# Retention and mixture-of-depths on one core: smaller loads, a one-pass rank, later weights, and a third MLP held back

## The chip, the cores and the metric

The kernel runs on one core of a Trainium2 chip. A core has five engines, each with its own stream of instructions: TensorE (PE, matrix products into PSUM; loads of its stationary operand are listed apart as PEld), VectorE (DVE), ScalarE (ACT), GpSimd (POOL) and SyncE (SP), which here only issues transfers. Sixteen DMA engines move data between HBM and the on-chip SBUF. The metric is the device time of one execution in microseconds (us), lower is better.

## The reference

Eight sequences of 576 tokens, 8 heads of width 64, everything in float32. First retention without a softmax, then a mixture of depths over the 512 channels that the heads form together: the 128 tokens of each sequence with the highest score pass through a two-layer MLP, weighted by a sigmoid of their score; the others stay as they are.

```python
scores = q @ k.T / sqrt(64)                     # per batch and head, 576x576
gamma  = 1 - 2.0 ** (-5 - arange(8))            # one decay a head
ret    = scores * where(i >= j, gamma ** (i - j), 0)
x      = (ret @ v) laid out as (8, 576, 512)
s      = x @ w_gate                             # one score a token
top    = the 128 tokens of a sequence with the highest s
out    = x;  out[top] += sigmoid(s[top]) * (relu(x[top] @ w1) @ w2)   # w1 512x1024, w2 1024x512
```

## The kernel before

**Tiling.** A sequence is cut into 9 chunks of 64 tokens. Two sequences, a pair, lie side by side on the 128 partitions (64 each), so there are 4 pairs of 9 chunks, 36 steps in all. The host packs for each step the transposed q, the transposed k, v and k into one row of 4 x 512 floats a partition, 1 MB a step.

**A retention step** (`s` counts them) does on PE, in 128 matmuls of 64x64: the scores of the chunk with itself (`sc_ps`, L142), the running state `u_ps` from k and v (L152), and for the chunk before it the product of masked scores and v (`y_ps`, L162) and of q and the state (L169). POOL scales v by the decay (`vs`, L130), DVE masks the scores (`am`, L185), scales the result (`xs`, L199) and forms the score with `wg` (L203); ACT copies the state out of PSUM (L192). SP stores `xs` (L205).

**Ranking.** When a pair is through, `spread` puts its 576 scores in a row on all partitions (L218, L222), `compare` counts per chunk on DVE how many scores of the row are higher (L228) and, in a second instruction over 64 to 576 columns, how many equal ones come before (L231); `one_hot` adds the two counts (L237) and compares them with 128 slots (L240). `fetch` turns that into row numbers on PE (`idx_ps`, L252, L253) and has POOL gather the chosen rows from the output in HBM (`xr`, L261); `gates` recomputes their scores (L274, L276).

**MLP.** A pair's MLP is cut into nine parts that wait in a list, `parts`: one `turn` (transposes, L289), four `up` (16 matmuls each, L300), four `down` (8 matmuls each, L312), the second and fourth of which end with the addition (L317) and POOL's scatter into the output (L319).

**Order.** The order of instructions on PE, DVE, ACT and SP is the order of the code. The last loop goes through the steps: a load six steps ahead, the step's matmuls, masks and stores, then one part from the list if there is one, then what `steps` holds for that step. For pair `p`, with `s = 9p + 10`, that is `spread` at `s`, three `compare` at each of `s`, `s+1`, `s+2`, `one_hot` at `s+2`, `fetch` at `s+3`, `gates` at `s+4`; the pair's nine parts join the list at `s+5`, so that the first is taken a step later. After step 36 there is no retention left. SP issues loads, weights and stores in one queue: `load(s+6)`, a weight matrix at two of the steps, then the store of step `s-1`, which waits for DVE. Loads have 8 buffers. The compiler gives the transfers issued by SP eight semaphores in turn, so a transfer waits until the one eight before it has landed.

Of the kernel before, what the change touches and what calls it, by code (L numbers as in the profile page):

```python
# [9 lines left out]
F32 = mybir.dt.float32  # L10
# [3 lines left out]
OP = mybir.AluOpType  # L14
PSUM = bass.MemoryType.PSUM

P = 128
C = 64
ET = mybir.EngineType
# [3 lines left out]
def layout(H, NC, cap):  # L23

    at, n = {}, 0
    for name, size in (("dec", 2 * NC * H), ("causal", C), ("ident", C), ("before", NC * C),
                       ("slots", cap), ("eye", P), ("place", 2 * NC + 2)):
        at[name] = n
        n += size
    at["end"] = n  # L30
    return at
# [3 lines left out]
def kernel(  # L35
# [22 lines left out]
    nc = tc.nc  # L58
# [32 lines left out]
    def load(s):  # L91
        x = loads.tile([P, 4, DM], F32, name="raw")
        nc.sync.dma_start(out=x, in_=qkvk[s].rearrange("p (a e) -> p a e", a=4))
        raw[s] = x

    ctx.enter_context(tc.manual_schedule(engines=ENGINES))
    load(0)
    table = const.tile([P, col["end"]], F32, name="table")
    n_first = col["ident"]
    nc.sync.dma_start(out=table[:, :n_first], in_=consts[:, :n_first])  # L100
    load(1)
    load(2)
# [10 lines left out]
    ident = table[:, col["ident"] : col["ident"] + C]  # L113
    before = table[:, col["before"] : col["before"] + NC * C]
    slots = table[:, col["slots"] : col["slots"] + cap]
# [95 lines left out]
    def spread(p):  # L211
        row[p] = work.tile([P, S], F32, name="row", bufs=2)
        for c0 in range(0, NC, 8):
            t = bank("row_ps")
            c1 = min(c0 + 8, NC)
            for c in range(c0, c1):
                for half in halves:
                    nc.tensor.matmul(  # L218
                        t[half, C * (c - c0) : C * (c - c0) + C],
                        sc[p][half, c : c + 1].to_broadcast([C, C]), ident[half, :],  # L220
                        start=True, stop=True, skip_group_check=True)
            nc.scalar.copy(out=row[p][:, C * c0 : C * c1], in_=t[:, : C * (c1 - c0)])  # L222
        rank[p] = work.tile([P, 2, NC], F32, name="rank", bufs=2)

    def compare(p, c):
        s = sc[p][:, c : c + 1]
        scr = work.tile([P, S], F32, name="scr2", bufs=1)
        nc.vector.tensor_scalar(scr, row[p], s, None, op0=OP.is_gt, op1=OP.add,  # L228
                                accum_out=rank[p][:, 0, c : c + 1])
        end = C * c + C  # L230
        nc.vector.scalar_tensor_tensor(  # L231
            scr[:, :end], row[p][:, :end], s, before[:, S - end :],
            op0=OP.is_equal, op1=OP.mult, accum_out=rank[p][:, 1, c : c + 1])

    def one_hot(p):
        r = work.tile([P, NC], F32, name="r", bufs=2)
        nc.vector.tensor_tensor(out=r, in0=rank[p][:, 0, :], in1=rank[p][:, 1, :], op=OP.add)  # L237
        hot[p] = work.tile([P, NC, cap], BF16, name="hot", bufs=nb)
        for c in range(NC):
            nc.vector.tensor_scalar(hot[p][:, c, :], slots, r[:, c : c + 1], None,  # L240
                                    op0=OP.is_equal)
# [97 lines left out]
    for p in range(NP):  # L339
# [6 lines left out]
        at(s + 4, gates, p)  # L346
        at(s + 5, mlp, p)

# [6 lines left out]
    for s in range(last + 1):  # L355
        if s + AHEAD < NS:
            load(s + AHEAD)
        if s == 4:
            nc.sync.dma_start(out=w1_sb, in_=w1.rearrange("(a p) f -> p a f", p=P))
        if s == 7:  # L360
            nc.sync.dma_start(out=w2_sb, in_=w2.rearrange("(a p) d -> p a d", p=P))
# [80 lines left out]
```

## Time and profile before

| | us |
|---|---|
| three runs | 299.83, 296.64, 299.77 (median 299.77) |
| the profiled execution | 298.31 |
| its span, first to last instruction | 296.5 |

| engine | busy us | share of the span |
|---|---|---|
| PE | 236.4 | 80% |
| PEld | 182.1 | 61% |
| DVE | 144.3 | 49% |
| POOL | 54.3 | 18% |
| ACT | 39.5 | 13% |

The profile is of one execution. Busy times are summed over instructions; matmuls are pipelined and their ends are modelled, so a busy PE need not be working at its peak. The mean clock granted to TensorE was 0.886 of full speed. In the lists an idle time is put down to whatever signal came last before it ended; "issue" means that the engine waited for nothing that the profile shows. A number in brackets after x counts instructions.

### The profile page before, as it was taken

What the parts mean: (1) busy time and instruction counts of PE and PEld (TensorE: products, weight loads), DVE (VectorE), ACT (ScalarE), POOL (GpSimd) and SP (SyncE); (2) the same over time, 40 slices, a digit from 0 to 9 for tenths busy, and PEclk for the clock granted to TensorE, in tenths of its full rate; (3) what the DMA queues carried; (4) which work ended last, traced back from release to release, by engine and by line L of the source; (5) the groups of instructions that cost most, each with busy time, mean ns of one, the idle gap of its engine ahead of it and who ended that gap; (6) DMA issues with size and microseconds to landing.
All of it is one profiled execution on the core that took longest, in us unless ns stands there. A gap on an engine that the chain in (4) does not pass through costs nothing.

```text
span 296.5 us, 10844 instructions
## 1 busy us (share of the span) xinstructions
PE 236.4 (80%) x4984; PEld 182.1 (61%) x4984; DVE 144.3 (49%) x361; ACT 39.5 (13%) x74; POOL 54.3 (18%) x56
## 2 busy tenths in 40 slices
PE   2575547555649889999799999988999994999992
PEld 2464447554547778875656888646568861468640
DVE  0152225346895834399754343996643089310011
ACT  1010001001100411310021122100220110011100
POOL 1231112211114212111242211113310000310011
PEclk9996577778655799999799999997999998799998
DMA  7999997997555898546396954112321100300000
GB/s 284 363 423 422 413 401 277 349 403 267 181 179 190 296 366 287 187 127 234 122 326 233 349 189 179 38 38 76 110 106 38 38 0 0 106 35 2 0 35 35
DMA packets 13693, 57.11 MB, mean 193 GB/s; under 512 B 1488, under 2 KB 1616, under 8 KB 9040
## 3 DMA queue, kind: packets, MB, share of 16 engines
q1 hardware_dynamic: 12368, 52.22, 47.4%
q0 software_dynamic: 1280, 4.20, 4.1%
q8 instruction: 39, 0.64, 0.8%
q14 instruction: 6, 0.05, 0.0%
HBM read 44.88 MB, written 11.53 MB: 190 GB/s over the span
## 4 chain that ended last, share of the span: by engine, by line
PE 55%; DVE 22%; issue 14%; DMA 5%; ACT 1%; SPq 1%; POOLq 0%; POOL 0%; DVEq 0%
PE h_ps L300 16%; PE ye_ps L312 10%; DVE scr L228 9%; PE sc_ps L142 7%; PE u_ps L152 7%; DVE scr L231 6%; PE y_ps L162 6%; PE y_ps L169 5%; DMA table<-in_consts 3%; DMA xr<-out,idx 2%; DVE am L185 2%; PE idx_ps L252 2%; PE row_ps L218 1%; DVE scr L203 1%; DVE xs L199 1%
## 5 line engine op out<-in xcount | busy, mean ns | idle before, releaser
L142 PE MATMUL sc_ps<-raw 64*64 64x64 f32 x1152 | 55.4, 255 | 15.6 <-issue 10.1
L162 PE MATMUL y_ps<-vs,am 64*64 64x64 f32 x1152 | 53.5, 253 | 16.7 <-DVE am L185 8.5
L130 POOL TENSOR_TENSOR vs<-raw,table 128x512 f32<-128x512 f32 x36 | 38.1, 1059 | 134.5 <-PE y_ps L162 81.0
L142 PEld LDWEIGHTS sc_ps<-raw 64*64 64x64 f32 x1152 | 49.2, 167 | 20.6 <-issue 15.0
L162 PEld LDWEIGHTS y_ps<-vs,am 64*64 64x64 f32 x1152 | 47.6, 164 | 21.4 <-issue 11.5
L312 PE MATMUL ye_ps<-w_sb,hT 128*128 128x512 f32 x128 | 59.4, 614 | 0.0
L300 PE MATMUL h_ps<-xg,w_sb 128*128 128x256 f32 x256 | 58.5, 384 | 0.7 <-ACT xg L290 0.7
L152 PE MATMUL u_ps<-vs,raw 64*64 64x64 f32 x1024 | 51.4, 259 | 7.9 <-issue 7.7
L300 PEld LDWEIGHTS h_ps<-xg,w_sb 128*128 128x128 f32 x256 | 47.6, 190 | 7.7 <-ACT xg L290 1.0
L152 PEld LDWEIGHTS u_ps<-vs,raw 64*64 64x64 f32 x1024 | 45.9, 171 | 9.9 <-issue 9.8
L169 PE MATMUL y_ps<-st,raw 64*64 64x64 f32 x1024 | 48.6, 252 | 4.2 <-issue 4.1
L169 PEld LDWEIGHTS y_ps<-st,raw 64*64 64x64 f32 x1024 | 43.1, 164 | 5.1 <-issue 5.1
L199 DVE TENSOR_TENSOR xs<-y_ps,table 128x512 f32<-128x512 f32 x36 | 24.8, 688 | 39.7 <-PE y_ps L169 39.7
L312 PEld LDWEIGHTS ye_ps<-w_sb,hT 128*128 128x128 f32 x128 | 24.2, 195 | 27.1 <-issue 26.4
L185 DVE TENSOR_TENSOR am<-sc_ps,table 128x512 f32<-128x512 f32 x36 | 24.8, 689 | 31.5 <-PE y_ps L162 21.2
L228 DVE TENSOR_SCALAR_CACHE_REDUCE scr<-row,sc 128x576 f32<-128x576 f32 x36 | 29.2, 812 | 20.2 <-ACT row L222 19.2
L192 ACT COPY st<-u_ps 128x512 f32<-128x512 f32 x32 | 18.8, 586 | 150.4 <-PE y_ps L169 120.6
L203 DVE SCALAR_TENSOR_TENSOR scr<-xs,wg 128x512 f32<-128x512 f32 x36 | 24.9, 692 | 1.2
L319 POOL DMA_INDIRECT out<-o,idx x8 | 8.1, 1011 | 93.9 <-DVE idx L257 52.4
L231 DVE SCALAR_TENSOR_TENSOR scr<-row,sc,table 128x64 f32<-128x64 f32 (+8 forms) x36 | 22.3, 620 | 1.3
L317 DVE SCALAR_TENSOR_TENSOR o<-ye_ps,gate,xr 128x512 f32<-128x512 f32 x8 | 6.0, 750 | 33.3 <-PE ye_ps L312 33.3
L302 ACT ACTIVATE hT<-h_ps 128x512 f32<-128x512 f32 x16 | 9.6, 598 | 57.6 <-PE h_ps L300 57.6
(27 smaller groups left out, 81.6 us busy)
## 6 DMA issues: line engine op xcount, KB each, us to landing
raw<-in_qkvk SPq DMA_DIRECT2D x36, 1024.0 KB, 6.7
out<-xs SPq DMA_DIRECT2D x36, 256.0 KB, 2.6
w_sb<-in_w SPq DMA_DIRECT2D x2, 2048.0 KB, 12.3
table<-in_consts SPq DMA_DIRECT2D x1, 458.0 KB, 9.5
wg<-in_w_gate SPq DMA_DIRECT2D x1, 256.0 KB
xr<-out,idx POOLq DMA_INDIRECT x8, 4.3
out<-o,idx POOLq DMA_INDIRECT x8, 2.8
table<-in_consts SPq DMA_DIRECT2D x1, 104.0 KB, 5.0
```

Source lines behind the costliest of these rows:

```text
L130: nc.gpsimd.tensor_tensor(out=heads(vs[s]), in0=heads(raw[s][:, 2, :]), in1=dec[:, 0, c, :].unsqueeze(2).to_broadcast([P, H, D]), op=OP.mult,)
L142: yield lambda h=h, half=half: nc.tensor.matmul(sc_ps[s][half, hd[h]], x[half, 1, hd[h]], x[half, 0, hd[h]], start=True, stop=True, skip_g ...
L152: yield lambda h=h, half=half: nc.tensor.matmul(u[half, hd[h]], x[half, 3, hd[h]], vs[s][half, hd[h]], start=c == 0 and h == 0, stop=c == ...
L162: yield lambda h=h, i=i, half=half: nc.tensor.matmul(y_ps[s][halves[1 - i], hd[h]], am[s][half, h, :], vs[s][half, hd[h]], start=h == 0, s ...
L169: yield lambda h=h, i=i, half=half: nc.tensor.matmul(y_ps[s][halves[1 - i], hd[h]], raw[s][half, 0, hd[h]], st[s - 1][half, hd[h]], start= ...
L185: nc.vector.tensor_tensor(out=am[s], in0=heads(sc_ps[s]), in1=causal.unsqueeze(1).to_broadcast([P, H, C]), op=OP.mult)
L199: nc.vector.tensor_tensor(out=heads(xs[s]), in0=heads(y_ps[s]), in1=dec[:, 1, c, :].unsqueeze(2).to_broadcast([P, H, D]), op=OP.mult)
L203: nc.vector.scalar_tensor_tensor(scr, xs[s], 1.0, wg, op0=OP.mult, op1=OP.mult, accum_out=sc[p][:, c : c + 1])
L228: nc.vector.tensor_scalar(scr, row[p], s, None, op0=OP.is_gt, op1=OP.add, accum_out=rank[p][:, 0, c : c + 1])
L231: nc.vector.scalar_tensor_tensor(scr[:, :end], row[p][:, :end], s, before[:, S - end :], op0=OP.is_equal, op1=OP.mult, accum_out=rank[p][: ...
L300: nc.tensor.matmul(t[:, a, :w], w1_sb[:, d, P * (f + a) : P * (f + a) + P], xg[group][:, d, :w], start=d == 0, stop=d == KD - 1)
L312: nc.tensor.matmul(ye[u][:m], hT[group][:, f, at : at + m], w2_sb[:, f, :], start=f == 0, stop=f == FB - 1)
```

## The change

Four things change. A step's load is issued as four transfers, one for each of the packed arrays, into the same tile (`load`); the first table of constants now goes ahead of the first load. The two instructions of `compare` become one `scalar_tensor_tensor` over all 576 columns, which subtracts the score and compares the difference with 0 or with minus 2**-125 from a table `ahead` (1,088 columns in place of 576); the addition in `one_hot` falls away. The loads of `w1` and `w2` are issued at steps 7 and 10 in place of 4 and 7. The parts of a pair join the list at `s+4` in place of `s+5`, except those of the third pair (`p == 2`), which join at step 36.

```diff
--- before.py
+++ after.py
@@ -15,6 +15,7 @@
 PSUM = bass.MemoryType.PSUM

 P = 128
+TINY = 2.0**-125
 C = 64
 ET = mybir.EngineType
 ENGINES = {ET.PE, ET.DVE, ET.Activation, ET.SP}
@@ -23,7 +24,7 @@
 def layout(H, NC, cap):

     at, n = {}, 0
-    for name, size in (("dec", 2 * NC * H), ("causal", C), ("ident", C), ("before", NC * C),
+    for name, size in (("dec", 2 * NC * H), ("causal", C), ("ident", C), ("ahead", (2 * NC - 1) * C),
                        ("slots", cap), ("eye", P), ("place", 2 * NC + 2)):
         at[name] = n
         n += size
@@ -90,14 +91,15 @@

     def load(s):
         x = loads.tile([P, 4, DM], F32, name="raw")
-        nc.sync.dma_start(out=x, in_=qkvk[s].rearrange("p (a e) -> p a e", a=4))
+        for a in range(4):
+            nc.sync.dma_start(out=x[:, a, :], in_=qkvk[s, :, a * DM : a * DM + DM])
         raw[s] = x

     ctx.enter_context(tc.manual_schedule(engines=ENGINES))
-    load(0)
     table = const.tile([P, col["end"]], F32, name="table")
     n_first = col["ident"]
     nc.sync.dma_start(out=table[:, :n_first], in_=consts[:, :n_first])
+    load(0)
     load(1)
     load(2)
     nc.sync.dma_start(out=table[:, n_first:], in_=consts[:, n_first:])
@@ -111,7 +113,7 @@
     dec = table[:, : 2 * NC * H].rearrange("p (s c h) -> p s c h", s=2, c=NC)
     causal = table[:, col["causal"] : col["causal"] + C]
     ident = table[:, col["ident"] : col["ident"] + C]
-    before = table[:, col["before"] : col["before"] + NC * C]
+    ahead = table[:, col["ahead"] : col["slots"]]
     slots = table[:, col["slots"] : col["slots"] + cap]
     eye = table[:, col["eye"] : col["eye"] + P]
     place = const.tile([P, NC + 1, 2], BF16, name="place")
@@ -220,24 +222,19 @@
                         sc[p][half, c : c + 1].to_broadcast([C, C]), ident[half, :],
                         start=True, stop=True, skip_group_check=True)
             nc.scalar.copy(out=row[p][:, C * c0 : C * c1], in_=t[:, : C * (c1 - c0)])
-        rank[p] = work.tile([P, 2, NC], F32, name="rank", bufs=2)
+        rank[p] = work.tile([P, NC], F32, name="rank", bufs=2)

     def compare(p, c):
-        s = sc[p][:, c : c + 1]
+
         scr = work.tile([P, S], F32, name="scr2", bufs=1)
-        nc.vector.tensor_scalar(scr, row[p], s, None, op0=OP.is_gt, op1=OP.add,
-                                accum_out=rank[p][:, 0, c : c + 1])
-        end = C * c + C
         nc.vector.scalar_tensor_tensor(
-            scr[:, :end], row[p][:, :end], s, before[:, S - end :],
-            op0=OP.is_equal, op1=OP.mult, accum_out=rank[p][:, 1, c : c + 1])
+            scr, row[p], sc[p][:, c : c + 1], ahead[:, (NC - 1 - c) * C :][:, :S],
+            op0=OP.subtract, op1=OP.is_gt, accum_out=rank[p][:, c : c + 1])

     def one_hot(p):
-        r = work.tile([P, NC], F32, name="r", bufs=2)
-        nc.vector.tensor_tensor(out=r, in0=rank[p][:, 0, :], in1=rank[p][:, 1, :], op=OP.add)
         hot[p] = work.tile([P, NC, cap], BF16, name="hot", bufs=nb)
         for c in range(NC):
-            nc.vector.tensor_scalar(hot[p][:, c, :], slots, r[:, c : c + 1], None,
+            nc.vector.tensor_scalar(hot[p][:, c, :], slots, rank[p][:, c : c + 1], None,
                                     op0=OP.is_equal)


@@ -344,7 +341,7 @@
         at(s + 2, one_hot, p)
         at(s + 3, fetch, p)
         at(s + 4, gates, p)
-        at(s + 5, mlp, p)
+        at(max(s + 4, NS) if p == NP - 2 else s + 4, mlp, p)

     AHEAD = 6
     for s in range(3, AHEAD):
@@ -355,9 +352,9 @@
     for s in range(last + 1):
         if s + AHEAD < NS:
             load(s + AHEAD)
-        if s == 4:
+        if s == 7:
             nc.sync.dma_start(out=w1_sb, in_=w1.rearrange("(a p) f -> p a f", p=P))
-        if s == 7:
+        if s == 10:
             nc.sync.dma_start(out=w2_sb, in_=w2.rearrange("(a p) d -> p a d", p=P))
         if s + 1 < NS:
             scaled(s + 1)
@@ -408,9 +405,9 @@
     table[:, : col["causal"]] = np.stack([1.0 / power, power / math.sqrt(D)], 1).reshape(P, -1)
     j = np.arange(C)
     table[:, col["causal"] : col["ident"]] = i[:, None] <= j[None, :]
-    table[:, col["ident"] : col["before"]] = i[:, None] == j[None, :]
-    table[:, col["before"] : col["slots"] - C] = 1.0
-    table[:, col["slots"] - C : col["slots"]] = j[None, :] < i[:, None]
+    table[:, col["ident"] : col["ahead"]] = i[:, None] == j[None, :]
+    table[:, col["ahead"] : col["ahead"] + S - C] = -TINY
+    table[:, col["ahead"] + S - C : col["ahead"] + S] = -TINY * (j[None, :] < i[:, None])
     table[:, col["slots"] : col["eye"]] = np.arange(cap)[None, :]
     table[:, col["eye"] : col["place"]] = np.eye(P)

```

**SP, from the first store on** (a transfer and what it waits for; DMAHW0 to DMAHW7 are the eight semaphores of its transfers). Before:

```order
L205 DMA out<-xs 128x512 [waits DMAHW3_49,DVE_49]
L93 DMA raw<-in_qkvk 128x2048 [waits DMAHW4_49,PE_49,Pool_49]
L205 DMA out<-xs 128x512 [waits DMAHW5_49,DVE_49]
L93 DMA raw<-in_qkvk 128x2048 [waits DMAHW6_49,PE_49,Pool_49]
L205 DMA out<-xs 128x512 [waits DMAHW7_49,DVE_49]
L93 DMA raw<-in_qkvk 128x2048 [waits DMAHW0_49,PE_49,Pool_49]
L359 DMA w_sb<-in_w 128x4x1024 [waits DMAHW1_49]
```

The same place in the changed kernel:

```order
L207 DMA out<-xs 128x512 [waits DMAHW3_49,DVE_49]
L95 DMA raw<-in_qkvk 128x512 [waits DMAHW4_49,PE_49,Pool_49]
L95 DMA raw<-in_qkvk 128x512 [waits DMAHW5_49]
L95 DMA raw<-in_qkvk 128x512 [waits DMAHW6_49]
L95 DMA raw<-in_qkvk 128x512 [waits DMAHW7_49]
L207 DMA out<-xs 128x512 [waits DMAHW0_49,DVE_49]
```

A load of one transfer has become four, each with the wait for the transfer eight before it; eight transfers now hold under two steps' loads, where they held about four steps' loads and stores.

**PE, where retention ends** (`sc_ps` to `y_ps` are retention, `xg_ps` the turn, `h_ps` and `ye_ps` the halves of the MLP, `row_ps` the spread of the fourth pair). Before, the end of step 35 and what follows up to the fourth pair's `idx_ps`:

```order
L142 MATMUL sc_ps<-raw 64x64 x2
L162 MATMUL y_ps<-vs,am 64x64 x2
L169 MATMUL y_ps<-st,raw 64x64 x16
L300 MATMUL h_ps<-xg,w_sb 128x256 x8
L162 MATMUL y_ps<-vs,am 64x64 x16
L169 MATMUL y_ps<-st,raw 64x64 x16
L300 MATMUL h_ps<-xg,w_sb 128x256 x16
L218 MATMUL row_ps<-table,sc 64x64 x18
L300 MATMUL h_ps<-xg,w_sb 128x256 x8
L312 MATMUL ye_ps<-w_sb,hT 128x512 x8
```

The same place in the changed kernel:

```order
L144 MATMUL sc_ps<-raw 64x64 x2
L164 MATMUL y_ps<-vs,am 64x64 x2
L171 MATMUL y_ps<-st,raw 64x64 x16
L164 MATMUL y_ps<-vs,am 64x64 x16
L171 MATMUL y_ps<-st,raw 64x64 x16
L286 MATMUL xg_ps<-table,xr 128x128 x8
L220 MATMUL row_ps<-table,sc 64x64 x18
L297 MATMUL h_ps<-xg,w_sb 128x256 x24
```

The third pair's turn and first `up` have moved behind the last retention matmul, and steps 33 to 35 have no part of an MLP between them; `idx_ps` of the fourth pair now follows the third `up`, and the last `up` and all `down` follow `idx_ps`.

**DVE, one step in which a pair is ranked** (`am`, `xs`, `scr,sc` are retention, `rank<-row` the comparison). Before:

```order
L185 TENSOR_TENSOR am<-sc_ps,table 128x512
L199 TENSOR_TENSOR xs<-y_ps,table 128x512
L203 SCALAR_TENSOR_TENSOR scr,sc<-xs,wg 128x512
L228 TENSOR_SCALAR scr_2681,rank<-row,sc 128x576
L231 SCALAR_TENSOR_TENSOR scr_2681,rank<-row,sc,table 128x256
L228 TENSOR_SCALAR scr_2684,rank<-row,sc 128x576
L231 SCALAR_TENSOR_TENSOR scr_2684,rank<-row,sc,table 128x320
L228 TENSOR_SCALAR scr_2687,rank<-row,sc 128x576
L231 SCALAR_TENSOR_TENSOR scr_2687,rank<-row,sc,table 128x384
```

In the changed kernel:

```order
L187 TENSOR_TENSOR am<-sc_ps,table 128x512
L201 TENSOR_TENSOR xs<-y_ps,table 128x512
L205 SCALAR_TENSOR_TENSOR scr,sc<-xs,wg 128x512
L230 SCALAR_TENSOR_TENSOR scr_2769,rank<-row,sc,table 128x576
L230 SCALAR_TENSOR_TENSOR scr_2771,rank<-row,sc,table 128x576
L230 SCALAR_TENSOR_TENSOR scr_2773,rank<-row,sc,table 128x576
```

Six instructions between two masks have become three.

## Rows read from the trace of the kernel before

**Rows 1.** The page, DMA queues: packets, MB, share of 16 engines.

```profile
q1 hardware_dynamic: 12368, 52.22, 47.4%
q8 instruction: 39, 0.64, 0.8%
```

**Rows 2.** The windows, stages of the span; the head names the columns.

```profile
core 0: us, PE busy (x) PEld busy (x) DVE busy (x) ACT busy (x) POOL busy (x), PEclk, DMA share, GB/s
0.00:73.20 73.20, 38.72 (x1367) 36.94 (x1367) 25.26 (x55) 7.86 (x13) 15.02 (x18) 0.81 0.94 365
73.20:99.20 26.00, 18.53 (x578) 16.75 (x580) 20.19 (x55) 3.63 (x5) 6.27 (x6) 0.57 0.56 189
228.74:296.50 67.76, 57.99 (x238) 36.84 (x238) 20.27 (x59) 6.37 (x13) 5.90 (x6) 0.93 0.08 28
```

**Rows 3.** The windows, from one restart of PE to the next.

```profile
19.39:25.84 6.45, 2.20 (x127) 2.07 (x127) 1.99 (x4) 0.59 (x1) 1.04 (x1) 0.88 1.01 419
25.84:32.11 6.27, 3.81 (x127) 3.62 (x127) 2.08 (x4) 0.59 (x1) 1.04 (x1) 0.50 1.02 418
44.67:48.49 3.82, 3.67 (x129) 3.58 (x128) 2.08 (x4) 0.59 (x1) 1.04 (x1) 0.55 0.53 218
54.39:61.37 6.98, 4.04 (x128) 3.85 (x128) 2.77 (x5) 0.00 (x0) 2.09 (x2) 0.76 1.02 389
66.83:73.19 6.36, 2.77 (x127) 2.64 (x127) 3.91 (x13) 1.29 (x3) 1.04 (x1) 0.92 0.83 303
73.19:76.87 3.68, 3.67 (x127) 3.50 (x127) 2.69 (x7) 0.59 (x1) 0.23 (x1) 0.50 0.16 56
```

**Rows 4.** The chain of waits in order of time: start us, us, what.

```profile
18.02 1.36 issue
...
21.59 4.25 issue
...
29.65 2.46 issue
```

**Rows 5.** DMA issues on the page: op, count, KB each, us to landing.

```profile
raw<-in_qkvk SPq DMA_DIRECT2D x36, 1024.0 KB, 6.7
out<-xs SPq DMA_DIRECT2D x36, 256.0 KB, 2.6
```

**Rows 6.** Groups by form: count | busy us, mean ns | idle before.

```profile
L228 DVE TENSOR_SCALAR_CACHE_REDUCE scr<-row,sc 128x576 f32<-128x576 f32 x36 | 29.2, 812 | 20.2 <-ACT row L222 19.2
L231 DVE SCALAR_TENSOR_TENSOR scr<-row,sc,table 128x576 f32<-128x576 f32 x4 | 3.3, 818 | 0.1
L231 DVE DVE_READ_ACCUMULATOR scr<-row,sc,table 128x1 f32 x36 | 2.9, 81 | 0.0
```

**Rows 7.** Group of the page, all forms of the second comparison together.

```profile
L231 DVE SCALAR_TENSOR_TENSOR scr<-row,sc,table 128x64 f32<-128x64 f32 (+8 forms) x36 | 22.3, 620 | 1.3
```

**Rows 8.** Timeline of DVE: start, us, instruction, idle before it and its releaser.

```profile
12.34 0.18 DVE L120 CAST place<-table 128x20 bf16<-128x20 f32 x1 [12.34 <-DMA table<-in_consts]
```

**Rows 9.** The windows, single steps between 99 and 229 us.

```profile
112.86:118.52 5.66, 5.66 (x113) 4.90 (x113) 2.28 (x5) 1.19 (x2) 1.03 (x2) 1.00 0.78 265
143.60:149.35 5.75, 4.66 (x131) 3.97 (x129) 3.10 (x8) 0.00 (x0) 2.45 (x3) 0.70 0.67 224
```

**Rows 10.** The chain of waits, MLP work of PE and the end.

```profile
112.86 3.65 PE h_ps L300 x16
...
161.72 1.02 PE xg_ps L289 x8
...
253.08 8.70 PE ye_ps L312 x16
...
277.46 6.88 PE ye_ps L312 x16
```

**Rows 11.** Waits of PE: waited for, us in total, times, longest.

```profile
PE idx_ps L252 <- DVE hot L240: 9.8, 4, 3.9
```

## The prediction, as put on record before the changed kernel's time was known

> **What bounds the kernel now.** I read the windows first, then the chain of waits, then the groups. By stage [rows 2] the first 73.2 us hold ten of the 36 steps and have the DMA engines busy at 0.94, while PE shows 38.7 us of work; this is the costliest stretch. It looks like a transfer limit, but it isn't one: loads run six steps ahead, and the chain there names no load as what PE waits for. It says "issue", that is nothing visible, for 1.4 to 4.3 us at a time [rows 4].
>
> Cutting the stretch where PE restarts shows what that is [rows 3]: each piece holds 127 to 129 matmuls and as many weight loads, some 256 instructions, whatever they are. The page has a queue named instruction with 39 packets and 0.64 MB [rows 1]: 16.4 KB a packet, and PE's 2 x 4984 instructions over 39 are 256 each. So I read the gaps as PE out of instructions until its next packet has come. A retention step is 4 x 32 matmuls with their weight loads, exactly one packet. [...]
>
> What a packet costs depends on what else the DMA engines carry [rows 3]. With DMA busy at 0.16 a piece takes 3.68 us, at 0.53 it takes 3.82, with loads in the way 6.27, and while the 2 MB of `w2` pass 6.98. The excess over 3.68 is 2.59 us with loads; 1 MB at the 418 GB/s of that row lasts 2.51 us. So the packet seems to wait for about one whole transfer in front of it, not for the whole queue: at 19.39 us SP had issued 10.5 MB and 17.4 us at 419 GB/s had moved 7.3, so 3.2 MB or 7.7 us were still queued, and that piece took 6.45 us, 2.77 over.
>
> From 99 us on the MLP parts fill the pieces (a step with an `up` is 5.66 us [rows 9], of which the `up` is 3.65 [rows 10], so retention alone is 2.01 on PE) and PE is the bound, except where it waits for the ranks: four times, 9.8 us in all, 3.9 at most [rows 11]. The tail after the last retention matmul is 67.76 us [rows 2].
>
> **The change, part by part.** The sum is against the profiled execution, 298.31 us, which is a span of 296.5 and 1.8 around it; the median of the three runs is 1.5 higher, inside their spread.
>
> *Loads in four.* Each transfer is 256 KB, 0.63 us at 418 GB/s. If a packet waits for one transfer, a piece becomes 3.68 + 0.63 = 4.31 us. Nine pieces lie between 19.39 and 73.19, 53.8 us together (the first and the last are in [rows 3]). One of them now meets `w1`; I give it the 6.98 us of the row with `w2`. 8 x 4.31 + 6.98 = 41.5: **-12.3 us**. Bounds: nine pieces of 3.68 are 33.1, -20.7 us; if the wait is for something that four transfers don't shorten, 6.27 stays and the gain is 0. I take the value near the better end, since the row with 0.53 is at 3.82. Two things speak for one transfer as the unit: the 2 MB one cost more than the 1 MB ones, and the wait did not grow with the queue. What the rows can't tell is whether the four transfers of a load count as one. [...] No row here shows the engines one by one.
>
> SP issues 144 loads in place of 36, at about 0.4 us each; with a store that is some 2 us a step against pieces of 4.31, so this is covered, and would show only in steps shorter than 2 us. The wait for the transfer eight before is now a wait with 2 MB in flight, 5 us of traffic, against 2.6 us to landing for a lone 256 KB store [rows 5]: covered too. Behind it the first store and `load(8)` go out some 4 us later than now, since SP must first get rid of the 32 initial pieces; `xs` has four buffers and `load(8)` is needed six pieces later, so nobody waits.
>
> At the start, DVE's first mask sits behind the cast of `place`, which waits for the second table until 12.34 us [rows 8]. That table grows by 512 columns, 256 KB, +0.63 us, and all bytes ahead of it come in rows of 2 KB, which ran at 389 in place of 419 GB/s [rows 3]: on 4 MB +0.7. Against that the gap of 1.36 us before the first restart [rows 4] goes. **0**, bounds -1.4 and +1.4.
>
> *Ranks in one pass.* A chunk costs now 812 + 620 ns and two accumulator reads of 81 [rows 6, 7], 1.59 us; the new instruction is that of the 576-column form, 818 + 81 = 0.90. Nine chunks: 6.2 us less on DVE for each pair, more than the longest of the four waits. **-9.8 us** on PE; bounds -9.8 and, if PE merely arrives earlier too, -5.
>
> [...] In the tail the 16 matmuls of `down` right behind the wait took 8.70 us, later ones 6.88 [rows 10]: **-1.8**.
>
> Between 73.2 and 99.2 us DVE holds the first pair's steps; 6.2 less 3.9 already counted leaves -2.3, but `w2` now passes here, 6.98 - 4.31 = 2.7: **+0.4**, bounds -2.3 and +2.7.
>
> *Weights later.* `w1` and `w2` are first read at steps 16 and 20, nine and ten steps after their issue, over 35 us: nobody waits for them. What they cost is counted above.
>
> *Third MLP held.* PE's matmuls stay the same; what counts is how many steps run bare, without a part. Steps 33 to 35 and half of 36 do now, and a bare step takes a packet's time, not 2.01: 3.5 x (3.68 - 2.01) = **+5.8** (no loads are left by then). Bounds: 0 if packets come faster, +8.0 at 4.31. Step 15 is no longer bare and takes the first pair's turn, 1.02 us [rows 10]: **-1.0**. In the tail the row of scores must wait for DVE's last two instructions, behind the turn: **+0.4**. Then three `up` (10.9 us) run while DVE does nine chunks and nine `hot`; by the ranks' 0.90 us that is as long, so `idx_ps` finds them ready, and the gather lands under the last `up` and four `down`.
>
> Sum: -12.3 + 0 - 9.8 - 3.7 - 1.8 + 0.4 + 5.8 - 1.0 + 0.4 = -22.0; 296.5 - 22.0 + 1.8 = **276.3**, so 276 us.
>
> **The rivals.**
>
> *Not relieved.* The four pieces of a load follow one another in one queue, and the packet waits for all of them as it did for one. Then 6.27 us a piece stay, and only the rest of the sum is left: 276.3 + 12.3 = 288.6. For it: the wait was never shorter than one load when a load was in front. Against: the row at 0.53.
>
> [...]
>
> *Small transfers starve the steps, slower than before.* Each has its own latency, 2.6 us by the store's row [rows 5]; were only two in the air at a time, five a step would take 6.5 us, 34 steps 221, and with the start of 19.4 and the tail of 67.8 the time were 308 + 1.8 = 310. [...] It decides from the point where fewer than 13/4.3 = 3 are in flight. Against: the semaphores allow eight, and `w2`, whose rows are of 2 KB, ran at 389 GB/s [rows 3].
>
> [...]
>
> **How the numbers follow.** The forecast (268 to 284) gets 0.55, fully relieved (256 to 268) 0.15, not relieved (284 to 292) 0.21, eaten up 0.04, starved 0.05. The range leaves out the lower half of the second and the last two cases: 263 to 290. About 1% is what a measurement of this kernel can tell from no change. Faster by more: 0.55 + 0.15 + 0.21 = 0.91; same 0.04; slower 0.05.
>
> **What would show it.** Right: pieces of 256 PE instructions between 20 and 60 us of 4 to 4.5 us with DMA above 0.8; still 39 instruction packets; step 10 over by some 60 us; 36 ranks of 0.82 us and no wait of `idx_ps` for `hot`; bare steps near the end of about 3.7 us each; a tail near 67 us. Wrong: pieces still at 6.3 us, or PE and POOL waiting for `raw` by name, which would be the starved case.

## The result, and the profile after

The changed kernel takes **285.12 us** (median of 4 runs, 284.86 to 285.88) beside 299.08 for the kernel before (296.64 to 299.83); the ratio is 0.955, with a 95% interval from 0.949 to 0.961. That is 14 us less. The prediction said 276, with a range from 263 to 290: the direction is right, the time lies in the range, and 9 us of the predicted gain are missing. The profiled execution took 284.86, its span is 283.1, the granted clock 0.917 on average where it was 0.886. Where executions of one kernel lie more than 1.5% apart, differences below are read from its fastest.

Transfers after, on the page; columns as in [rows 1]:

```profile
q1 hardware_dynamic: 27920, 52.49, 54.0%
q8 instruction: 39, 0.64, 0.9%
```

The packets of the transfers have more than doubled, the instruction packets are 39 as before. The pieces of 256 PE instructions and the stages, in the windows of the changed kernel; columns as in [rows 2]:

```profile
22.81:28.17 5.36, 2.21 (x128) 2.07 (x128) 2.00 (x4) 0.58 (x1) 1.04 (x1) 0.95 1.05 386
38.71:44.71 6.00, 3.68 (x127) 3.49 (x127) 2.09 (x4) 0.58 (x1) 1.04 (x1) 0.50 1.00 374
55.52:61.54 6.02, 3.77 (x127) 3.69 (x128) 2.69 (x5) 0.00 (x0) 2.08 (x2) 0.76 1.02 395
67.29:74.28 6.99, 3.90 (x127) 3.71 (x127) 3.73 (x7) 1.28 (x3) 1.23 (x1) 0.59 0.96 324
0.00:99.37 99.37, 56.85 (x1951) 52.72 (x1951) 41.69 (x90) 11.66 (x19) 21.65 (x24) 0.78 0.92 325
99.37:217.85 118.48, 110.54 (x2774) 83.48 (x2774) 70.31 (x156) 19.64 (x39) 29.19 (x26) 1.00 0.59 196
217.85:283.09 65.24, 59.19 (x262) 39.60 (x262) 15.23 (x40) 8.03 (x16) 5.86 (x6) 0.98 0.08 29
```

The pieces were to come down to 4.31 us. Without a weight matrix they take 4.9 to 6.0; the one before `w1` has landed takes 6.02 (SP's wait for it ends at 62 us), and the two while `w2` is under way (issued at 66.76, landed by 79.2) take 6.99 and 6.17. The nine from 22.81 to 74.28 take 51.5 us, with `w1` and the first part of `w2`; before, the nine took 53.8 with both, and 41.5 were predicted. The last three rows are the time up to step 16, from there to the end of retention, and the tail. The first two of them before:

```profile
0.00:99.10 99.10, 57.15 (x1940) 53.59 (x1943) 45.35 (x107) 11.49 (x18) 21.29 (x24) 0.74 0.84 319
99.10:228.74 129.64, 121.22 (x2819) 91.67 (x2812) 78.70 (x196) 21.65 (x43) 27.12 (x26) 0.97 0.51 182
```

So the first stage has not gained, the middle one 11.2 us, the tail 2.5 (65.24 for 67.76 in [rows 2]).

DVE's first instructions, in the timeline of the changed kernel; columns as in [rows 8]:

```profile
15.56 0.18 DVE L122 CAST place<-table 128x20 bf16<-128x20 f32 x1 [15.56 <-DMA table<-in_consts]
15.64 0.69 DVE L187 TENSOR_TENSOR am<-sc_ps,table 128x512 f32<-128x512 f32 x1
```

And what stands ahead of that in its chain of waits:

```profile
3.06 4.94 DMA raw<-in_qkvk
8.02 7.51 DMA table<-in_consts
```

The first mask comes 3.2 us later than in [rows 8]. SP could not issue the second table until 8.02, since the transfer eight before it, a quarter of a load, had to land first; then the table took 7.51 us to come.

What PE waited for, longest kinds and the last; columns as in [rows 11]:

```profile
PE y_ps L171 <- issue: 11.9, 12, 3.1
PE sc_ps L144 <- issue: 11.0, 6, 3.5
...
PE idx_ps L249 <- DVE hot L237: 0.2, 1, 0.2
```

The waits for the ranks [rows 11] are gone, 9.8 us to 0.2; the "issue" waits have stayed, 30.0 us over the retention matmuls before and 35.9 now. POOL, in its own list, waits for `raw` by name, 5.0 us before and now

```profile
POOL vs L132 <- DMA raw<-in_qkvk: 18.8, 5, 6.4
```

The prediction named that as a sign of the starved case. It isn't that case: PE waits for POOL's `vs` once, 0.3 us, and for `raw` once, at the start. The groups of the comparison, by form:

```profile
L230 DVE SCALAR_TENSOR_TENSOR scr<-row,sc,table 128x576 f32<-128x576 f32 x36 | 35.8, 994 | 14.2 <-ACT row L224 13.3
L230 DVE DVE_READ_ACCUMULATOR scr<-row,sc,table 128x1 f32 x36 | 2.9, 82 | 0.0
```

A chunk takes 0.99 + 0.08 us on average, not 0.90, beside 1.59 before [rows 6, 7].

### The profile page after: what moved, and what is told of

The parts are those of the page before. It is cut to its first block, busy times and chain, and to the rows that moved or that the text cites. A ratio compares the mean times of both kernels' runs of the same rounds, so it can differ in the third digit from the quotient of the medians.

```text
span 283.1 us, 10883 instructions
## 1 busy us (share of the span) xinstructions
PE 226.6 (80%) x4984; PEld 175.8 (62%) x4984; DVE 127.2 (45%) x285; ACT 39.3 (14%) x74; POOL 56.7 (20%) x56
## 4 chain that ended last, share of the span: by engine, by line
PE 72%; issue 15%; DMA 7%; DVE 3%; SPq 1%; POOLq 0%; ACT 0%; POOL 0%; DVEq 0%
PE h_ps L297 20%; PE ye_ps L309 18%; PE sc_ps L144 10%; PE u_ps L154 10%; PE y_ps L164 6%; PE y_ps L171 5%; DMA table<-in_consts 3%; DMA xr<-out,idx 2%; DMA raw<-in_qkvk 2%; PE row_ps L220 2%; DVE scr L230 1%; PE xg_ps L286 1%; PE idx_ps L249 1%; DVE am L187 1%; SPq L95 1%
## 5 line engine op out<-in xcount | busy, mean ns | idle before, releaser
L144 PE MATMUL sc_ps<-raw 64*64 64x64 f32 x1152 | 52.8, 249 | 16.7 <-issue 11.0
L132 POOL TENSOR_TENSOR vs<-raw,table 128x512 f32<-128x512 f32 x36 | 39.5, 1098 | 125.0 <-PE y_ps L164 70.2
L164 PE MATMUL y_ps<-vs,am 64*64 64x64 f32 x1152 | 51.8, 247 | 15.4 <-issue 8.2
L144 PEld LDWEIGHTS sc_ps<-raw 64*64 64x64 f32 x1152 | 47.2, 161 | 24.4 <-issue 18.7
L171 PE MATMUL y_ps<-st,raw 64*64 64x64 f32 x1024 | 48.3, 243 | 12.3 <-issue 11.9
L309 PE MATMUL ye_ps<-w_sb,hT 128*128 128x512 f32 x128 | 57.4, 599 | 0.0
L164 PEld LDWEIGHTS y_ps<-vs,am 64*64 64x64 f32 x1152 | 45.9, 158 | 16.6 <-issue 9.3
L154 PE MATMUL u_ps<-vs,raw 64*64 64x64 f32 x1024 | 49.7, 248 | 5.5 <-issue 4.8
L154 PEld LDWEIGHTS u_ps<-vs,raw 64*64 64x64 f32 x1024 | 43.0, 160 | 12.2 <-issue 11.7
L230 DVE SCALAR_TENSOR_TENSOR scr<-row,sc,table 128x576 f32<-128x576 f32 x36 | 35.8, 994 | 14.2 <-ACT row L224 13.3
L258 POOL DMA_INDIRECT xr<-out,idx x8 | 7.9, 990 | 37.8 <-DVE idx L254 36.6
```

What stands on the lines that cost most here:

```text
L132: nc.gpsimd.tensor_tensor(out=heads(vs[s]), in0=heads(raw[s][:, 2, :]), in1=dec[:, 0, c, :].unsqueeze(2).to_broadcast([P, H, D]), op=OP.mult,)
L144: yield lambda h=h, half=half: nc.tensor.matmul(sc_ps[s][half, hd[h]], x[half, 1, hd[h]], x[half, 0, hd[h]], start=True, stop=True, skip_g ...
L154: yield lambda h=h, half=half: nc.tensor.matmul(u[half, hd[h]], x[half, 3, hd[h]], vs[s][half, hd[h]], start=c == 0 and h == 0, stop=c == ...
L164: yield lambda h=h, i=i, half=half: nc.tensor.matmul(y_ps[s][halves[1 - i], hd[h]], am[s][half, h, :], vs[s][half, hd[h]], start=h == 0, s ...
L171: yield lambda h=h, i=i, half=half: nc.tensor.matmul(y_ps[s][halves[1 - i], hd[h]], raw[s][half, 0, hd[h]], st[s - 1][half, hd[h]], start= ...
L230: nc.vector.scalar_tensor_tensor(scr, row[p], sc[p][:, c : c + 1], ahead[:, (NC - 1 - c) * C :][:, :S], op0=OP.subtract, op1=OP.is_gt, acc ...
```

## The experiments

Ratios are to the kernel before, run beside each on the same chip. An edit is against the changed kernel, except in e9, e11 and e12, where it is against the kernel before.

### What the instruction packets wait for: e8, e6, e7, e1

**e8_eight_loads**: from step 8 on no load, the tiles of the first eight steps are used again (28 MB left out, so the result is not the reference's).

```diff
     def load(s):
+        if s >= 8:
+            raw[s] = raw[s % 8]
+            return
```

> The changed kernel, but only the first eight steps are loaded; steps 8 to 35 work on the tiles of steps 0 to 7 again, so 28 MB of loads are left out (the result is another one). Theory A, PE waits for its instruction packets and these wait behind loads: with the DMA engines nearly empty after some 30 us, pieces of 256 PE instructions between 35 and 70 us take 3.5 to 3.8 us, except where w1 and w2 pass. Theory B, the pace of the first 70 us is set by the chain from PE to DVE to POOL and back: pieces stay at 5 to 6 us.

Measured: 271.9 us, one execution. Five pieces in the windows of e8, the last with `w1`:

```profile
28.36:31.89 3.53, 3.45 (x127) 3.45 (x127) 1.18 (x2) 0.59 (x1) 1.04 (x1) 0.52 0.49 184
31.89:35.88 3.99, 2.26 (x139) 2.09 (x131) 2.29 (x6) 0.59 (x1) 1.04 (x1) 1.00 0.37 136
35.88:39.87 3.99, 2.14 (x127) 2.00 (x127) 2.08 (x4) 0.59 (x1) 1.04 (x1) 1.00 0.20 70
39.87:43.31 3.44, 2.14 (x127) 2.01 (x127) 2.08 (x4) 0.59 (x1) 1.04 (x1) 1.00 0.15 47
43.39:49.96 6.57, 2.15 (x127) 2.02 (x128) 2.08 (x4) 0.59 (x1) 1.04 (x1) 0.92 1.00 341
```

Without a load a piece takes 3.4 to 4.0 us; one weight matrix puts it back at 6.57, though PE's own work in it is the same (2.15 us) and the granted clock is 0.92 where it was 1.00. So what PE waits for does come behind transfers, and the whole kernel is 13 us shorter without the loads. That it is an instruction packet rests on the count of 256 [rows 3]; no view shows a packet land.

**e6_one_2k_rows**: the step's load as one transfer of 1 MB, in rows of 2 KB instead of 8 KB, which tells the transfer's size from the length of its rows.

```diff
-        for a in range(4):
-            nc.sync.dma_start(out=x[:, a, :], in_=qkvk[s, :, a * DM : a * DM + DM])
+        nc.sync.dma_start(out=x, in_=qkvk[s].rearrange("a p e -> p a e"))
```

> The changed kernel with a load as one transfer again, but laid out in HBM so that its rows are 2 KB, as in the four transfers. If the size of a row decides how long an instruction packet waits, pieces between 23 and 50 us stay at 4.9 to 6.0 us as in the changed kernel (mean 5.4); if the size of a transfer or the bytes in flight decide, they go back to about 6.3 us.

Measured: 287.32 us, one execution; from 22.0 us on two pieces of 6.6 and 6.3 us, then 4.4 to 6.1 without a weight matrix. The first two are as long as before the change, so shorter rows alone do not shorten the wait.

**e7_four_8k_rows**: four transfers again, each of 32 partitions with rows of 8 KB.

```diff
+        for i in range(4):
+            part = slice(32 * i, 32 * i + 32)
+            nc.sync.dma_start(out=x[part], in_=qkvk[s, part].rearrange("p (a e) -> p a e", a=4))
```

> The changed kernel with four transfers a load, but each covers 32 partitions in rows of 8 KB, so transfers and bytes in flight are those of the changed kernel and the rows those of before. If the size of a row decides, pieces between 23 and 50 us go to about 6.3 us; if transfers or bytes in flight decide, they stay at a mean of 5.4 us.

Measured: 330.23 us, one execution. Six pieces in one window:

```profile
30.00:80.00 50.00, 21.86 (x759) 20.78 (x759) 11.81 (x23) 3.52 (x6) 6.25 (x6) 0.57 1.02 248
```

The DMA engines count as fully busy and move 248 GB/s where 374 to 386 stand in the rows of after; pieces take 7.7 to 9.1 us. The form of the transfer changed its rate, so this run tells nothing on the question; it only shows that this cut by partitions is a bad one.

**e1_one_load**: the split alone undone, one 1 MB transfer a step.

```diff
-        for a in range(4):
-            nc.sync.dma_start(out=x[:, a, :], in_=qkvk[s, :, a * DM : a * DM + DM])
+        nc.sync.dma_start(out=x, in_=qkvk[s].rearrange("p (a e) -> p a e", a=4))
```

> The changed kernel with each load as one transfer of 1 MB again. Theory A: the split shortened the pieces from 6.0 to 5.7 us, nine of them 2.3 us in all, but cost 3.2 us at the start, because SP must wait for landed transfers before it can issue the second table; without the split the mask of step 0 comes back to some 12.5 to 13.5 us, pieces go back to 6.0 and the time is 284 to 286, no different from the changed kernel. Rival: the split is worth most of the gain, and without it the time is above 292.

Measured: 286.89 us (283.59 to 287.75), ratio 0.958 [0.936, 0.981], no different from the changed kernel. The interval is wide, but had the split been worth the 12 us of the prediction, the ratio without it would be near 0.996. The nine pieces, from 20.22 to 73.22, take 53.0 us, 1.5 more than in the changed kernel, and the first mask comes earlier again (the cast of `place` at 13.1 us, not 15.56). The split, the prediction's largest term, is worth nothing that shows in the whole time.

### One edit undone or moved: e2, e3, e4, e5

**e2_place_late**: the cast of `place` goes from ahead of the loop to step 5.

```diff
     scaled(0)
-    constants()
...
+        if s == 5:
+            constants()
```

> The changed kernel with one edit: the cast of `place` (constants) moves from ahead of the first mask to step 5. In the changed kernel DVE's first mask waits for the second table until 15.56 us (12.34 before), and the restarts of PE are 3.4 us later than before. Theory A (the second table sets the start): the first mask comes as soon as the first scores are there, some 8 us, the first crossing of a 256-instruction piece falls from 17.1 us by 3 to 6 us, and as the pieces behind it keep their 5 to 6 us the whole kernel gets 3 to 6 us faster, 279 to 282. Rival B (the start is bound by loads or instruction packets anyway, the table's wait only stands last): first crossing earlier by under 1.5 us or the pieces longer by as much, 284 to 286.

Measured: 282.43 us, ratio 0.946 [0.940, 0.953]. DVE's first row in its timeline:

```profile
7.83 0.69 DVE L187 TENSOR_TENSOR am<-sc_ps,table 128x512 f32<-128x512 f32 x1 [7.83 <-PE sc_ps L144]
```

The mask now waits for PE's scores alone and comes 7.8 us earlier. Some 3 of these 8 us are left at the end, and nine pieces behind it take 53.3 us, not 51.5, which fits loads that still have to pass. The time lies between the two theories, just above A's 279 to 282, and the interval overlaps that of the changed kernel: that the start waited for the table is shown, the 3 us are at the edge of what can be told.

**e3_no_hold**: the third pair's parts join the list at `s+4` like the others.

```diff
-        at(max(s + 4, NS) if p == NP - 2 else s + 4, mlp, p)
+        at(s + 4, mlp, p)
```

> The changed kernel with only the third pair's hold undone: its nine MLP parts join the list at s+4 like the others, so steps 32 to 36 take parts and the tail holds fewer of them. Theory A (sum of the prediction): the hold made 3.5 bare steps (11.4 us measured, +4.4 over PE's work) and bought cover for the ranking of the fourth pair. Without it the steps get 4.4 us cheaper, and the fourth pair's ranking in the tail is covered by less MLP work: PE has the row of scores, then at most two or three parts of the third pair, and waits for DVE's nine comparisons (about 9 us) and the gather (a few us). Net +1 to +8 us, 286 to 293. Rival B (the hold is worth nothing because the parts left in the list cover the ranking anyway): 280 to 283, faster than the changed kernel.

Measured: 290.4 us, ratio 0.975 [0.964, 0.985]; theory A. The four executions lie at 286.6, 288.3, 292.5 and 293.3, those of the changed kernel at 284.9 to 285.9, and the profiled spans are 284.8 and 283.1; so with the parts at `s+4`, holding them back pays some 2 us, and that it pays more is not shown. PE's waits in e3 show one reason (0.4 and 0.7 us in the changed kernel):

```profile
PE xg_ps L286 <- DMA xr<-out,idx: 1.3, 2, 1.0
PE h_ps L297 <- ACT xg L287: 1.3, 1, 1.3
```

The fourth pair's gather has too little work over it, and the 64 matmuls of `up` behind these waits take 15.51 us in the chain, at a granted clock of 0.91, where 14.08 at 1.00 stand in the chain of the changed kernel.

**e4_weights_early**: `w1` at step 4 and `w2` at step 7, as before.

```diff
-        if s == 7:
+        if s == 4:
...
-        if s == 10:
+        if s == 7:
```

> The changed kernel with only the weights' place undone: w1 at step 4 and w2 at step 7, as before. Theory A (each 2 MB transfer holds up about one instruction packet wherever it passes): same time, 284 to 287; the pieces with 6 to 7 us move three steps earlier. Rival B (late weights are worth something: the early steps are bound by bytes and 4 MB more there take 10 us, while later they fall between loads): 288 to 295.

Measured: 283.74 us, ratio 0.951 [0.944, 0.958]; the interval overlaps that of the changed kernel. The spans are 283.9 and 283.1. Moving the weights gives nothing that can be told.

**e5_two_pass**: the two instructions of `compare` and the addition are back.

```diff
-        nc.vector.scalar_tensor_tensor(
-            scr, row[p], sc[p][:, c : c + 1], ahead[:, (NC - 1 - c) * C :][:, :S],
-            op0=OP.subtract, op1=OP.is_gt, accum_out=rank[p][:, c : c + 1])
+        nc.vector.tensor_scalar(scr, row[p], s, None, op0=OP.is_gt, op1=OP.add,
+                                accum_out=rank[p][:, 0, c : c + 1])
+        end = C * c + C
+        nc.vector.scalar_tensor_tensor(
+            scr[:, :end], row[p][:, :end], s, before[:, S - end : S],
+            op0=OP.is_equal, op1=OP.mult, accum_out=rank[p][:, 1, c : c + 1])
```

> The changed kernel with only the ranking undone: two instructions a chunk and the addition again (1.59 us a chunk where the one pass takes 1.07 with its accumulator read, as measured). Theory A (the ranking gives most of the gain): idx_ps waits for hot again, two or three times 2 to 4 us inside retention; with the cold step behind each it is 6 to 13 us slower than the changed kernel, 291 to 298. Rival B (the ranking was covered once the order changed; the gain comes from hold and packets): under 3 us slower, 285 to 288.

Measured: 305.16 us, ratio 1.022 [1.014, 1.029]: 20 us slower than the changed kernel, and slower than the kernel before. Theory A's cause, with 7 us more than the upper end of its 291 to 298. The wait, and the stages (to step 16, to the end of retention, tail):

```profile
PE idx_ps L255 <- DVE hot L243: 12.8, 4, 3.7
```

```profile
0.00:101.96 101.96, 59.67 (x1951) 55.94 (x1951) 47.20 (x111) 11.90 (x21) 21.56 (x24) 0.70 0.90 316
101.96:231.38 129.42, 117.14 (x2774) 87.62 (x2774) 79.68 (x192) 19.44 (x38) 27.27 (x26) 0.95 0.54 180
231.38:304.23 72.85, 63.08 (x262) 42.00 (x262) 20.46 (x59) 7.81 (x16) 5.87 (x6) 0.94 0.07 26
```

Against the stages of after there are 12.6 us more of waits, and the clock is lower in all three (0.70, 0.95 and 0.94 where 0.78, 1.00 and 0.98 were granted), by which PE's busy time grows by 13.3 us, partly where it would have been idle. The tail alone is 7.6 us longer, which theory A had left out: three `up` no longer cover nine chunks. So the other three edits without the ranking make the kernel slower.

### One edit alone: e9 and e12

**e9_ranks_only**: the kernel before with the one-pass ranking and nothing else (the edit in `compare`, `one_hot` and the table, as in the diff of the change).

> The kernel before with one edit alone, the one-pass ranking (and its wider table); loads in one transfer, weights and MLP parts as before. Undoing the ranking in the changed kernel cost 20 us, more than the prediction's three terms for it (9.8 + 3.7 + 1.8 = 15.3). Theory A (the terms are right in the old order): 15 us faster than before, 282 to 286, about as fast as the changed kernel with all four edits, whose other three then cancel. Rival B (ranking and order work together: only with the parts moved to s+4 and the hold does the one pass pay): 6 to 10 us faster, 289 to 293.

Measured: 281.28 us, ratio 0.945 [0.936, 0.954]; three of the four executions took 281.1 to 281.3, the other 449.85. Nearest theory A: one of the four edits does all that the four do together. By the medians it does 4 us more, but the intervals of the two ratios overlap. Its stages in the windows:

```profile
0.00:95.36 95.36, 54.93 (x1942) 51.71 (x1944) 41.12 (x90) 11.46 (x19) 21.82 (x24) 0.80 0.87 336
95.36:218.36 123.00, 116.52 (x2820) 89.18 (x2812) 72.70 (x156) 21.48 (x43) 29.70 (x27) 0.97 0.54 191
218.36:279.44 61.08, 54.91 (x239) 35.63 (x238) 15.04 (x40) 6.25 (x13) 5.89 (x6) 0.98 0.09 31
```

**e12_ranks_split**: e9 with the split and the first table ahead of the loads.

```diff
+    table = const.tile([P, col["end"]], F32, name="table")
...
     load(0)
...
-        nc.sync.dma_start(out=x, in_=qkvk[s].rearrange("p (a e) -> p a e", a=4))
+        for a in range(4):
+            nc.sync.dma_start(out=x[:, a, :], in_=qkvk[s, :, a * DM : a * DM + DM])
```

> The kernel before with the one-pass ranking and the changed kernel's loads (four transfers a step, the first table ahead of them); weights and MLP parts as before. Theory A (the split costs at the start what it gives in the pieces: first mask some 3 us later than with ranks alone, nine pieces 2 us shorter): 281 to 284, as ranks alone or up to 3 above. Rival B (the split gives what the prediction said, 12 us, and the weights or the hold take it back): 268 to 274.

Measured: 280.04 us, ratio 0.946 [0.940, 0.952], as e9 and near theory A. The nine pieces at the place of [rows 3] as one window, of e9 and then of e12, and the cast of `place` in each timeline:

```profile
19.44:73.04 53.60, 29.34 (x1143) 28.06 (x1142) 21.69 (x42) 5.38 (x10) 10.62 (x10) 0.77 0.96 376
```

```profile
22.28:74.72 52.44, 29.82 (x1142) 28.58 (x1143) 20.88 (x40) 5.39 (x10) 10.63 (x10) 0.77 1.02 367
```

```profile
12.57 0.18 DVE L121 CAST place<-table 128x20 bf16<-128x20 f32 x1 [12.57 <-DMA table<-in_consts]
```

```profile
15.30 0.18 DVE L122 CAST place<-table 128x20 bf16<-128x20 f32 x1 [15.30 <-DMA table<-in_consts]
```

With the same two weight matrices in them the nine pieces take 53.60 us in one transfer a step and 52.44 in four: the split gives 1.2 us, and costs 2.7 at the start. Step 16 begins at 95.36 and 95.78, and the spans are 279.4 and 277.6, within what two executions differ by.

### Fewer loads queued, and the fastest: e10 and e11

**e10_ahead3**: e2 with loads three steps ahead in place of six (`AHEAD = 3`).

> The changed kernel with the place cast at step 5 and loads issued three steps ahead in place of six; the same transfers and bytes, only fewer of them queued at any time. Theory A (an instruction packet waits for load bytes that are in flight; the first 60 us are full because loads run ahead of need, not because they are needed): pieces of 256 PE instructions fall from 5.5 to 6.3 us toward 4 to 4.5 from the second on, as where steps were not loaded at all (3.4 to 4.0), the first 80 us shrink by 6 to 12 us, and the whole is 270 to 277. Rival B (each step's own burst of four transfers holds up the packet, however few steps are queued): pieces stay at 5 to 6 us, the whole stays at 280 to 284; if PE or POOL comes to wait for raw by name, slower than that.

Measured: 280.42 us (275.79 to 281.83). No ratio is on record. Its nine pieces, and those of e2 at the same place:

```profile
15.97:63.29 47.32, 29.07 (x1142) 27.55 (x1143) 21.26 (x44) 5.38 (x10) 11.46 (x11) 0.75 0.97 347
```

```profile
15.67:68.94 53.27, 31.22 (x1142) 29.72 (x1143) 21.83 (x44) 5.39 (x10) 12.30 (x11) 0.68 1.01 367
```

Both numbers lie in theory B's bands, but pieces of 5.26 us against 5.92 suggest that the queued loads count for some of the wait, a step's own for more (the changed kernel's nine, with six loads ahead like e2's, take 51.5). Of these 6 us 3.4 are left between the two spans (276.4 and 279.8); the executions spread too widely to tell more.

**e11_best**: e9 with `AHEAD = 3`, the cast at step 5 and the first table ahead of `load(0)`; one transfer a step.

> The kernel before with the one-pass ranking, the place cast at step 5, the first table ahead of the first load and loads three steps ahead; loads in one transfer, weights at steps 4 and 7 and MLP parts at s+5 as before, so none of the changed kernel's other three edits. Theory A (ranking, start and prefetch depth are what pays): the ranking alone took 281.3; the earlier start is worth some 3, fewer queued loads some 2 to 6: 272 to 278, the fastest of all. Rival B (with loads in one transfer a shallow prefetch makes POOL wait for raw, and w1 and w2 at steps 4 and 7 get in its way): 279 to 284.

Measured: 279.49 us, ratio 0.942 [0.935, 0.949], the best ratio of all, just clear of the changed kernel's interval (0.949 to 0.961), not of that of e9. The time lies in theory B's band, and POOL does wait for `raw`, as B said; in e9 it waits 2.9 us:

```profile
POOL vs L131 <- DMA raw<-in_qkvk: 41.7, 11, 7.1
```

But PE's list has no wait for `vs`, and one for `raw`, at the start, so that this reaches PE is not shown. With one transfer a step the shallow queue gives little: nine pieces from 17.41 to 70.06 us take 52.65, and 53.60 in e9. The first mask comes at 8.22 where it came at 12.65 in e9; the spans are 278.1 and 279.4, no further apart than two executions of one kernel.

## Why the prediction was right or wrong

The time lies in the range, but not for the prediction's reason: the range had been drawn wide enough to take in part of the rival *not relieved*. The forecast band of 268 to 284 was missed, and the largest term of the sum did not come. That 285 is inside is luck as far as the loads go, and right as far as the ranks go.

By its own terms, in us; "measured" is a difference of spans, stages or pieces in two profiles, as named.

| term | predicted | measured |
|---|---|---|
| ranks: waits -9.8, steps at a low clock -3.7, tail -1.8, 73 to 99 us -2.3 | -17.6 | -17.1 (span 296.5 to 279.4 in e9) |
| loads in four, nine pieces | -12.3 | -1.2 (e12 against e9) |
| loads in four, start | 0 | +2.7 (the same) |
| loads in four, all that follows | 0 | -3.3 (the same; no mechanism shown, and none of it in the ratios) |
| `w2` in 73 to 99 | +2.7 | -0.8 (spans, after against e4) |
| hold: bare steps +5.8, turn in step 15 -1.0, row +0.4 | +5.2 | +6.3 (spans, e4 against e12, which differ by the parts alone) |

Each row rests on single profiles, and the spans of one kernel's executions differ by up to 3.5 us (e12: 276.7 to 280.2). By the ratios, each with an interval of some 2 to 3 us either way, the ranks give -16.5, the split +0.2, the order of the parts +1.5 and the weights +1.3: only the ranks are clear of noise.

**The ranks** were right as a mechanism and, summed, as a size. By stages e9 gains 3.7 us up to step 16, 6.6 to the end of retention and 6.7 in the tail. No wait of `idx_ps` for `hot` is left in e9, and the granted clock, 0.70 in the step behind the second pair's wait before [rows 9], is 1.00 in all eight windows of e9 between 105 and 194 us; PE's busy time in the middle stage falls from 121.2 to 116.5 us for the same work. The duration of the new instruction was taken at 0.90 and is 1.07, which the margin of 6.2 us on the longest wait of 3.9 hid. No run shows the -3.7 of the sum; what the runs show in its place is 2.5 us: the retention steps right behind the second and third pairs' `idx_ps` took 5.75 and 5.71 us before (from 143.60 and 201.94 us), at a granted clock of 0.70 and 0.71, and 4.54 and 4.45 us in the changed kernel (from 143.72 and 198.30 us), at 1.00.

**Loads in four** is the step that failed: "if a packet waits for one transfer, a piece becomes 3.68 + 0.63 = 4.31 us". That loads are the cause of the gaps is shown by e8, and that they are PE without instructions is the reading that fits their period of 256. That one transfer is the unit is not so. A piece costs nearly the same whether 1 MB comes in one transfer or four (5.96 and 5.83 us on average in e9 and e12, 5.89 and 5.72 in e1 and the changed kernel); what counts is whether a step's load is there (3.4 to 4.0 us in e8, mostly 4.9 to 6.5 elsewhere) and, in part, how much more is queued (e10, 5.26 us a piece against 5.92 in e2). That is the rival *not relieved*, "the packet waits for all of them as it did for one", with 288.6 us; it had 0.21. Its "against", the row with DMA at 0.53 and 3.82 us [rows 3], was read as a half-loaded state near which small transfers would lie. But PE worked for 3.67 of these 3.82 us, at a granted clock of 0.55: the row is PE's own work at the low clock, as is the 3.68 below it, and bounds the packet's wait only from above. The floor of 3.68 held all the same (3.4 to 4.0 in e8, where PE's work is 2.1 at full clock). Most likely the packet of such a piece passed between two loads, as in the second of these three of e9, in the windows, between its neighbours:

```profile
37.90:44.36 6.46, 3.29 (x128) 3.09 (x127) 2.08 (x4) 0.58 (x1) 1.04 (x1) 0.56 1.04 417
44.36:48.71 4.35, 3.69 (x128) 3.58 (x127) 2.08 (x4) 0.58 (x1) 1.04 (x1) 0.50 0.71 291
48.71:55.16 6.45, 2.20 (x127) 2.06 (x127) 2.08 (x4) 0.58 (x1) 1.04 (x1) 0.99 0.98 340
```

The middle one has the lower clock and more PE work, and is 2.1 us shorter; that this is chance of place was read from the alternation and not tested by a run of its own. The other support, that the 2 MB transfer cost more than the 1 MB ones, holds for `w2` alone: SP issues `w1`, of the same size, at 29.65 us before the change, and no piece from there to 54.39 us is longer than 6.28, no more than a 1 MB load costs.

Why the four count as one stays open, since no view shows the order within an engine.

**The start** failed on a queue that the text had looked at elsewhere. It counted the wait for the transfer eight before for the first store and for `load(8)` and found that nobody waits; the second table stands in the same queue, behind 12 pieces, and DVE's first mask behind that. The chain (8.02, 7.51) and e2 show it.

**Weights and hold.** The order of the parts costs by the spans, as predicted, and not beyond noise by the ratios; e4 can't tell the weights' part from nothing. The bare steps, 3.5 from 206.40 to 217.85 us, take 11.4 against 7.0 of PE's work, +4.4 where +5.8 stood. What e3 adds: the hold mends what moving the parts to `s+4` breaks. With the parts at `s+5` and the ranks in one pass neither is needed (spans of 277.6 us in e12 and 279.4 in e9, 283.9 in e4 and 283.1 in the changed kernel).

The measured column adds up to -13.4, from 296.5 to 283.1; the predicted one to -22.0. Of the missing 8.6 us, 10.5 are the loads in four and 0.5 the ranks; weights and order together cost 5.5, 2.4 less than was put down for them.

## What to carry to other kernels

Before cutting a transfer in four, test with the transfers gone and with the transfers whole: the first says what there is to win, the second whether the size is what holds it. When transfers are split, count them through the issuing queue up to the last one that somebody needs early, since a wait for the transfer n before becomes four times as near (here the second table could go out only at 8.02 us, and the first mask came 3.2 us later). And when several edits come together, run the likeliest one alone: here, by the ratios, it was worth all of the gain.

## What the runs showed of the hardware

The one-pass comparison has two times. In the changed kernel's timeline of DVE:

```profile
77.28 0.81 DVE L230 SCALAR_TENSOR_TENSOR scr<-row,sc,table 128x576 f32<-128x576 f32 x1
78.14 1.47 DVE L230 SCALAR_TENSOR_TENSOR scr<-row,sc,table 128x576 f32<-128x576 f32 x1
79.65 0.82 DVE L230 SCALAR_TENSOR_TENSOR scr<-row,sc,table 128x576 f32<-128x576 f32 x1
```

And POOL's at the same time:

```profile
77.74 1.25 POOL L132 TENSOR_TENSOR vs<-raw,table 128x512 f32<-128x512 f32 x1 [5.56 <-DMA out<-xs]
```

Of the 36, nine took 1.47 to 1.70 us, and each of the nine began while a `vs` was running or within 0.03 us of its start. A comparison in the middle of which a `vs` began took 0.81 or 0.82, as the first one here, and then it was the `vs` that was longer, 1.23 to 1.52 us where 1.03 is the shortest. The nine of the tail, where POOL has no `vs`, took 0.82 each. So of two that overlapped, the one that began second took longer in all but two cases, by 0.65 us a comparison and by 0.2 to 0.5 a `vs`. The two comparisons of 1.70 us are recorded as starting 0.02 and 0.03 us ahead of their `vs` and were the longer ones all the same, while those `vs` took 1.05. That the overlap is the cause is read from the times alone; no run takes it away.

Cutting a load by partitions (e7) took the rate from 374 to 386 GB/s down to 248 with the DMA engines as busy, the largest effect of any run here (one execution; why it is so was not tested).
